# Joining the 64-row tail products of two DFT stages to passes that are row-tiled already, and spreading the filler work anew

## The chip, the core and the metric

The kernel runs on one core of a Trainium2 chip. The metric is the device time of one execution in microseconds (us); lower is better. The median of three runs of the kernel before is 507.38 us (507.01 to 507.38).

## What is computed

```python
xn = layernorm(x)                       # x: [2048, 576]
s  = irfft2(rfft2(xn) * (w_r + 1j*w_i)) # branch A
z  = gelu(xn @ w_in)                    # branch B, w_in: [576, 4608]
z1, z2 = z[:, :2304], layernorm(z[:, 2304:])
g  = w_sp @ z2 + b_sp[:, None]          # w_sp: [2048, 2048]
out = x + s * silu((z1 * g) @ w_out)    # w_out: [2304, 576]
```

## The kernel before

**Stages.** Rows of x come in 16 blocks of 128 (`m`). Branch A is a chain of small matrix products: p0 (row DFT, 16 blocks), then through DRAM p1 and p2/p3 (column DFT, filter, its inverse), p4 and p5 (inverse row DFT, 16 pieces `j`). Branch B makes z2 (96 chunks of 128 x 384, kept in SBUF, normalized there) and z1 (72 chunks of 128 x 512, sent to DRAM), and then the main products `w_sp @ z2` in a Strassen-like scheme of seven products (P1 to P7) a unit, 27 units, with the output products after each third of the rows. The main products begin with `tsum`, differences of normalized z2 blocks, and need `slab_sums`, sums and differences of four transposed slabs of w_sp.

**Filling.** The order on SP, PE (TensorE) and DVE (VectorE) is the program's own, written out by hand (`tc.manual_schedule`); ACT (ScalarE) and POOL (GpSimd) are ordered by the scheduler. `fill(n)` puts n z chunks between the steps of branch A, so that PE always has something to do; the string `kinds` says for each place whether it is a z2 chunk ("2") or a z1 chunk ("1"). `fill`'s second argument (`pace`) says how many items of the queue of z2 statistics and norms DVE takes after each chunk. After p5 come the chunks that are left, with the slab sums among them, and then `main`.

**Tails.** The inner dimension is 576 = 4 x 128 + 64. A chunk is four full-height products and one of 64 rows. Tails of four chunks are made together in one pass (place 1 of every four): two chunks are finished by it and two are begun by it, and partners lie in the upper and the lower 64 rows of the array, so two 64-row products can run beside one another. p0 and p5 have such a remainder too (288 = 2 x 128 + 32 rows, two parts; 289 = 2 x 128 + 33), but make it with a third product of full height, whose dead rows are zero in the tables (`live`, `seen`).

**Around the change, with lines.** `xpose` (L283) transposes a normalized block on PE (L287) and ACT copies it to `xnT` (L288). `p0_fold` (L292) adds and subtracts halves on DVE; `p0` (L297) makes six products (L302), ACT evacuates them (L304), POOL sends them to DRAM. Statistics of a block are `ln1` (L254: DVE L259/L260, reciprocal root on ACT for blocks 0 and 1, on POOL after that, `rstd_of` L248/L250), `ln1_apply` (L276/L279) normalizes it. z2 chunks are L410 on PE and L423/L429 on ACT; for the blocks in `ACT_SUMS` (4, 6, 8, 12, 14) ACT makes the sums for the norm too (a square over two chunks, L426). z1 chunks are L495/L504. `p5` (L381) has six products (L385), ACT and DVE evacuate (L388, L390, L391), POOL sends the piece to DRAM (L393). Norms are L466, slab sums L481 (one of the four, `SLB[6]`, on POOL for the first third), tsum L542/L544 on DVE and L546 on POOL. PSUM has four one-bank buffers for z chunks and transposes (`psh`) and two of two banks for branch A (`psa`).

Of the kernel before, what the change touches and what calls it, by code (L numbers as in the profile page):

```python
# [14 lines left out]
P = 128  # L15
# [8 lines left out]

def build_consts(S, D, L, LC0):
    tp = 2.0 * np.pi
    H = D // 2
    LE = L - L // 2
    d = np.zeros((3, P))
    live = np.ones((3, P))  # L30
    for b in range(2):
        d[b] = b * P + np.arange(P)
    nt_ = H - 2 * P
    d[2, 0:nt_] = 2 * P + np.arange(nt_)
    d[2, nt_:2 * nt_] = H + d[2, 0:nt_]
    live[2, 2 * nt_:] = 0.0
    cd = np.zeros((P, 2, 3, 2, LE))
    for par in range(2):
        l = 2 * np.arange(LE) + par
        ang = tp * ((d[:, :, None] * l) % D) / D * 1.0  # L40
        wt = live[:, :, None] * (l < L)
        cd[:, par, :, 0, :] = (np.cos(ang) * wt).transpose(1, 0, 2)
        cd[:, par, :, 1, :] = (-np.sin(ang) * wt).transpose(1, 0, 2)
    cd = cd.reshape(P, -1)

    s1 = np.arange(N1)
    k1 = np.arange(N1)
    lo, hi = k1 // N2, k1 % N2
    pos = [4 * hi + 2 * c + lo for c in range(2)]
    g1 = np.zeros((N2, P, P))  # L50
    g4 = np.zeros((N2, P, P))
    for s2 in range(N2):
        th = -tp * (((s1[:, None] * k1[None, :]) % N1) / N1 + s2 * k1[None, :] / S)
        co, si = np.cos(th), np.sin(th)
        for c, c2, v in ((0, 0, co), (1, 0, -si), (0, 1, si), (1, 1, co)):
            g1[s2, c * N1 + s1[:, None], pos[c2][None, :]] = v
        cot, sit = co.T, -si.T
        for c, c2, v in ((0, 0, cot), (1, 0, -sit), (0, 1, sit), (1, 1, cot)):
            g4[s2, pos[c][:, None], c2 * N1 + s1[None, :]] = v
    m2 = np.zeros((P, P))  # L60
    m3 = np.zeros((P, P))
    a = np.arange(N2)
    th = -tp * ((a[:, None] * a[None, :]) % N2) / N2
    co, si = np.cos(th), np.sin(th)
    for lo_ in range(2):
        for c, c2, v in ((0, 0, co), (1, 0, -si), (0, 1, si), (1, 1, co)):
            m2[c * N1 + lo_ * N2 + a[:, None], c2 * N1 + 2 * a[None, :] + lo_] = v
        for c, c2, v in ((0, 0, co), (1, 0, si), (0, 1, -si), (1, 1, co)):
            m3[c * N1 + 2 * a[:, None] + lo_, c2 * N1 + lo_ * N2 + a[None, :]] = v
    m3j = np.concatenate([m3[N1:], -m3[:N1]], axis=0)  # L70
    mm = np.stack([m2, m3, m3j], axis=1).reshape(P, 3 * P)

    ceso = np.zeros((P, len(LC0), 2, L))
    dd = np.arange(L)[None, :]
    seen = 0
    for i, l0 in enumerate(LC0):
        lv = (l0 + np.arange(P))[:, None]
        th = tp * ((lv * dd) % D) / D
        cl = np.where((lv == 0) | (lv == D // 2), 1.0, 2.0) * (lv >= seen) * 0.5 / (S * D)
        ceso[:, i, 0, :] = cl * np.cos(th)  # L80
        ceso[:, i, 1, :] = -cl * np.sin(th)
        seen = l0 + P
    return dict(cdsd=cd, g1=g1.transpose(1, 0, 2).reshape(P, N2 * P), g4=g4.transpose(1, 0, 2).reshape(P, N2 * P),
                mm=mm, ceso=ceso.reshape(P, -1))

@with_exitstack
def kernel(
# [23 lines left out]
    LC0 = [0, P, L - P]  # L111
    NLC = len(LC0)
# [6 lines left out]
    C = build_consts(S, D, L, LC0)  # L119
# [27 lines left out]
    nc.scalar.dma_start(out=ident[:], in_=cd_id.ap())  # L147
# [6 lines left out]
    nc.gpsimd.tensor_scalar(out=one[:], in0=one[:], scalar1=1.0, scalar2=1.0, op0=ALU.add, op1=ALU.mult)  # L154
# [59 lines left out]

    def load_x(c):
        t = AIN[c][:, 0:4 * D].rearrange("p (m d) -> p m d", m=4)
        if c == 0:
            for i in range(4):
                nc.sync.dma_start(out=t[:, i, :], in_=xv[:, i, :])
                if i == 1:  # L220
                    nc.sync.dma_start(out=CDSD, in_=cd_cdsd.ap().rearrange("p (a k l) -> p a k l", a=2, k=3))
        else:
            nc.sync.dma_start(out=t, in_=xv[:, 4 * c:4 * c + 4, :])
        return t
# [4 lines left out]
    def load_win(t, fs):  # L229
        for a in range(2):  # L230
            nc.sync.dma_start(out=t[:, a:KS - 1:2, :], in_=wv[a, 0:2 * P, fs].rearrange("(b p) f -> p b f", p=P))
        for q in range(4):
            nc.sync.dma_start(out=t[q * HT:(q + 1) * HT, KS - 1, :], in_=wv[q % 2, 2 * P:H2, fs])
# [6 lines left out]
    XC = [load_x(0)]  # L240
    for g in range(3):
        load_win(WIN2[:, :, 2 * g * ZC:2 * (g + 1) * ZC], slice(Fh + 2 * g * ZC, Fh + 2 * (g + 1) * ZC))
        XC.append(load_x(g + 1))
    nc.sync.dma_start(out=G1, in_=cd_g1.ap().rearrange("p (s k) -> p s k", s=N2))

    def rstd_of(mv, n, tag):
        ve = small.tile([P, n], F32, tag=tag + "v")
        nc.gpsimd.tensor_scalar(out=ve[:], in0=mv[:, :, 1], scalar1=1e-5, scalar2=1.0, op0=ALU.add, op1=ALU.mult)  # L248
# [4 lines left out]
    def ln1(ms):  # L253
        n = len(ms)  # L254
        mv = small.tile([P, n, 2], F32, tag=f"mv{n}", bufs=5)
        for i, m in enumerate(ms):
            st = small.tile([P, 2, 6], F32, tag="st1", bufs=4)
            for h in range(2):
                nc.vector.bn_stats(out=st[:, h, :], in_=XC[m // 4][:, m % 4, h * H2:(h + 1) * H2])  # L259
            nc.vector.bn_aggr(out=mv[:, i, :], in_=st[:])  # L260
        if ms[0] < 2:
            rs = small.tile([P, n], F32, tag=f"l1{n}r", bufs=5)
            nc.scalar.activation(out=rs[:], in_=mv[:, :, 1], func=ACT.Sqrt, bias=eps[:], scale=1.0)
            nc.vector.reciprocal(out=rs[:], in_=rs[:])
        else:
            rs = rstd_of(mv, n, f"l1{n}")
        for i, m in enumerate(ms):
            ln1_of[m] = (mv[:, i, 0:1], rs[:, i:i + 1])

    ln1_of = {}  # L270
# [26 lines left out]
    def p0(m):  # L297
        pa = psa.tile([P, 2, 512], F32, tag="a")
        for par in range(2):
            for k in range(3):  # L300
                lhs = FS[m % 4][:, par, k, :] if k < 2 else xnT[:, m, KS - 1, :]
                nc.tensor.matmul(pa[:, par, 0:2 * LE], lhsT=lhs, rhs=CDSD[:, par, k, :], start=(k == 0), stop=(k == 2))  # L302
        sg = PST[m % 8].rearrange("p (c l) -> p c l", c=2)
        nc.scalar.activation(out=sg.rearrange("p c (l a) -> p a c l", a=2),  # L304
                             in_=pa[:, :, 0:2 * LE].rearrange("p a (c l) -> p a c l", c=2), func=ACT.Identity)
# [59 lines left out]
    def p4(u):  # L365
        ch, lc = u // NLC, u % NLC
        av = AIN[ch].rearrange("p (s l) -> p s l", s=8)
        pa = psa.tile([P, 2, 4, P], F32, tag="a")
        for i in range(8):
            nc.tensor.matmul(pa[:, i // 4, i % 4, :], lhsT=av[:, i, LC0[lc]:LC0[lc] + P], rhs=G4[:, ch * 8 + i, :],  # L370
# [10 lines left out]
    def p5(j):  # L381
        pa = psa.tile([P, 2, 512], F32, tag="a")
        for c in range(2):
            for lc in range(NLC):
                nc.tensor.matmul(pa[:, c, 0:L], lhsT=V[:, lc, c, 2 * j:2 * j + 2, :], rhs=CESO[:, lc, c, :],  # L385
                                 start=(lc == 0), stop=(lc == NLC - 1))
        ob = THF[:, j % 2 * L:(j % 2 + 1) * L]
        nc.scalar.activation(out=ob, in_=pa[:, 1, 0:L], func=ACT.Identity)  # L388
        y = YST[j % 8]
        nc.vector.tensor_tensor(out=y[:, 0:L], in0=pa[:, 0, 0:L], in1=ob, op=ALU.add)  # L390
        nc.vector.tensor_tensor(out=y[:, L:D], in0=pa[:, 0, H2 - 1:0:-1], in1=ob[:, H2 - 1:0:-1], op=ALU.subtract)  # L391
        for h in range(2):
            nc.gpsimd.dma_start(out=Yv[2 * j + h], in_=y[h * N1:(h + 1) * N1, :])  # L393
# [77 lines left out]
    SA = dict(P1=4, P2=1, P5=2, P4=3, P6=0, P7=5, P3=6)  # L471
# [6 lines left out]
    def slab_sums(i, it):  # L478
        for o, a, b, op in ((5, 4, 2, ALU.subtract), (2, 2, 3, ALU.add), (0, 2, 4, ALU.subtract), (6, 1, 0, ALU.subtract)):
# [158 lines left out]
    kinds = "2" * (MT + 12) + "2221" * 4 + "2" * 12 + "12112111" * 6 + "21" * 12 + "2212" * 3 + "22112221"  # L638
# [11 lines left out]
    def fill(n, pace=1):  # L650
        for _ in range(n):
# [5 lines left out]
            if i % 4 == 1:  # L657
                done = held[:]
                held[:] = [chunk(i + 1), chunk(i + 2)]
                for r, c in enumerate(sorted(done + held, key=lambda c: c.wide)):  # L660
                    c.mm(KS - 1, slice(r % 2 * KT, (r % 2 + 1) * KT), c in held, c in done)
            elif i % 4 >= 2:
# [9 lines left out]
            z2_stats(pace)  # L672

    SP, PE, DVE = mybir.EngineType.SP, mybir.EngineType.PE, mybir.EngineType.DVE
    with tc.manual_schedule(engines={SP, PE, DVE}):
# [9 lines left out]
        ln1([0])  # L685
        ln1_apply(0)
        xpose(0)
        keep_warm(2)
        ln1([1])
        ln1_apply(1)  # L690
        nc.scalar.activation(out=THF[:, 0:1], in_=ln1_of[1][0], func=ACT.Gelu_apprx_tanh)
        p0_fold(0)
        xpose(1)
        ln1([2])
        p0(0)
        fill(1, 0)
        ln1_apply(2)
        p0_fold(1)
        fill(1, 0)
        xpose(2)  # L700
        p0(1)
        ln1([3])
        ln1_apply(3)
        fill(1, 0)
        nc.sync.dma_start(out=MM, in_=cd_mm.ap().rearrange("p (a k) -> p a k", a=3))
        ln1([4])
        for m in range(2, MT):
            if m + 1 < MT:
                xpose(m + 1)
            p0_fold(m)  # L710
            if m + 3 < MT:
                ln1([m + 3])
            if m + 2 < MT:
                ln1_apply(m + 2)
            fill(1, 0)
            p0(m)
# [5 lines left out]
        fill(11, 2)  # L722
        for s2 in range(0, N2, 2):
            p1(s2)
            fill(1)
# [6 lines left out]
        fill(12, 2)  # L732
        p2(0)
        for hh in range(0, N2, 2):
            fill(2)
            if hh + 2 < N2:
                p2(hh + 2)
            fill(1)
# [3 lines left out]
        fill(12, 2)  # L742
        for u in range(4 * NLC):
            p4(u)
            fill(1)
        for j in range(MT):
            p5(j)
            if j < 4 * NT // P:
                load_slab(0, (0, 2, 1, 3)[j % 4], j // 4)
            fill(1)  # L750
        load_z1(0)
        rest = kinds.rindex("2") + 1 - place[0]
        for i in range(NT // P):
            fill(rest // 4, 2)
            slab_sums(i, 0)
        fill(rest - 3 * (rest // 4), 3)
# [55 lines left out]
```

## Time and profile before

| | |
|---|---|
| time of the profiled execution | 507.27 us |
| its span on the core | 505.5 us |
| median of the runs | 507.38 us |
| PE, DVE, ACT, POOL busy | 98%, 65%, 34%, 43% of the span |
| p0 stage, waits for p1's input | until 41.5, until 50.7 us |
| p1; p2/p3; p4; p5 | from 50.7; 68; 147; 164 us |
| chunks that are left, after p5 | 191 to 212 us |
| main and output products | 212 to 500 us |

Busy times are unions of an engine's instructions. Matmuls are pipelined: an instruction lasts longer than its step, so what one costs is read from start to start in the timeline.

### The profile page before, as it was taken

The numbers are of one execution on the slowest core, as the hardware profiler recorded it, in microseconds if no ns is written. First come the engines' busy times: TensorE is split into PE (matmuls) and PEld (weight loads), VectorE is DVE, ScalarE is ACT, GpSimd is POOL, SyncE is SP. The second block draws the span as 40 slices with busy tenths as digits, with TensorE's granted clock in tenths as the row PEclk, the third lists the DMA queues.
The fourth block names the chain that finished last, engine by engine and source line by source line (L and its number), as shares of the span: only waits on it lengthen the run. The fifth ranks groups of instructions, "written<-read, shape, count | busy, mean of one in ns | idle before, by whom it ended". The sixth has DMA issues, their size and how long they took to land.

```text
span 505.5 us, 9339 instructions
## 1 busy us (share of the span) xinstructions
PE 497.5 (98%) x3454; PEld 313.8 (62%) x3454; DVE 329.6 (65%) x712; ACT 171.1 (34%) x356; POOL 217.5 (43%) x285
## 2 busy tenths in 40 slices
PE   7999999999999999999999999999999999999997
PEld 3565554444456664466666677666666678888885
DVE  5998887546355576766656547866665637877734
ACT  5887887556668666500000001100000011000001
POOL 2772243433332686754453511435445301666600
PEclk9999999999999999999999999999999999999999
DMA  8964869878573994381211399211121673111302
GB/s 257 333 180 132 281 216 325 248 209 238 164 267 93 178 276 151 126 272 33 63 32 47 92 169 209 75 47 48 31 64 31 150 140 120 34 43 44 88 18 79
DMA packets 85950, 70.82 MB, mean 140 GB/s; under 512 B 39760, under 2 KB 78416, under 8 KB 85648
## 3 DMA queue, kind: packets, MB, share of 16 engines
q1 hardware_dynamic: 80608, 56.08, 42.1%
q0 software_dynamic: 5152, 14.11, 8.4%
q8 instruction: 27, 0.44, 0.4%
q14 instruction: 19, 0.16, 0.1%
q10 hardware_dynamic: 144, 0.03, 0.0%
HBM read 40.55 MB, written 21.26 MB: 122 GB/s over the span
## 4 chain that ended last, share of the span: by engine, by line
PE 93%; DVE 4%; DMA 1%; issue 1%; ACT 1%; POOL 0%; SPq 0%; DVEq 0%; ACTq 0%
PE pm L558 43%; PE ph L495 14%; PE po L612 13%; PE ph L410 12%; PE pa L385 2%; PE pb L356 2%; PE pa L302 1%; PE pa L370 1%; PE pa L320 1%; PE pa L344 1%; PE pw L679 1%; DVE st L259 1%; DMA AR<-Ad 1%; PE pt L287 1%; DVE AR L276 1%
## 5 line engine op out<-in xcount | busy, mean ns | idle before, releaser
L558 PE MATMUL pm<-AR,Z_74 128*128 128x384 bf16 (+1 forms) x864 | 138.8, 308 | 0.0
L562 DVE TENSOR_TENSOR AR<-pm,AR 128x384 f32<-128x384 f32 (+3 forms) x162 | 82.5, 513 | 74.1 <-PE pm L558 70.0
L558 PEld LDWEIGHTS <-Z_74 128*128 128x128 bf16 x864 | 84.5, 98 | 40.6
L558 PE MATMUL pm<-AR 128*128 128x384 bf16 (+1 forms) x648 | 107.0, 308 | 0.1
L410 PE MATMUL ph<-AR 128*128 128x384 bf16 (+1 forms) x480 | 89.4, 327 | 0.5 <-DMA AR<-in_B_w_in_dram 0.4
L495 PE MATMUL ph<-AR 128*128 128x512 bf16 (+1 forms) x360 | 85.2, 379 | 0.0
L558 PEld LDWEIGHTS <-AR 128*128 128x128 bf16 x648 | 63.4, 98 | 30.7 <-issue 0.3
L572 ACT ACTIVATE AR<-pm 128x384 f32<-128x384 f32 (+1 forms) x27 | 12.3, 454 | 185.4 <-PE pm L558 185.4
L612 PE MATMUL po<-AR 128*128 128x288 bf16 x540 | 66.6, 286 | 0.0
L612 PEld LDWEIGHTS <-AR 128*128 128x128 bf16 x594 | 56.9, 98 | 13.9
L546 POOL TENSOR_TENSOR AR<-Z_74,AR 128x1024 bf16<-128x1024 bf16 x27 | 57.8, 2142 | 14.0 <-PE pm L558 12.1
L410 PEld LDWEIGHTS <-AR 128*128 128x128 bf16 (+1 forms) x480 | 39.8, 97 | 37.2 <-issue 17.7
L515 POOL DMA_DIRECT2D Z1d<-AR x58 | 32.9, 568 | 65.1 <-ACT AR L504 60.9
L573 POOL TENSOR_TENSOR AR<-AR 128x384 f32<-128x384 f32 (+1 forms) x27 | 22.8, 845 | 78.1 <-ACT AR L572 78.1
L504 ACT ACTIVATE AR<-ph 128x512 bf16<-128x512 f32 x72 | 42.5, 596 | 16.9 <-PE ph L495 14.1
L495 PEld LDWEIGHTS <-AR 128*128 128x128 bf16 (+1 forms) x360 | 30.5, 97 | 28.5 <-issue 4.6
L429 ACT ACTIVATE Z_74<-ph 128x384 bf16<-128x384 f32 x66 | 30.8, 492 | 20.0 <-PE ph L410 19.8
L615 ACT ACTIVATE TH<-po 128x576 f32<-128x576 f32 x15 | 9.8, 651 | 77.8 <-PE po L612 77.8
L576 POOL TENSOR_TENSOR AR<-AR 128x384 f32<-128x384 f32 (+1 forms) x27 | 30.3, 1123 | 11.8 <-DVE AR L562 11.8
L569 DVE TENSOR_TENSOR AR<-AR 128x384 bf16<-128x384 bf16 (+1 forms) x108 | 31.7, 335 | 0.9
L346 DVE TENSOR_TENSOR AR<-pa,AR 128x578 bf16<-128x578 f32 x32 | 22.7, 751 | 13.6 <-PE pa L344 13.6
L621 DVE SCALAR_TENSOR_TENSOR AR<-TH,po 128x576 bf16<-128x576 f32 x15 | 11.3, 752 | 29.9 <-ACT TH L615 29.9
(105 smaller groups left out, 492.1 us busy)
## 6 DMA issues: line engine op xcount, KB each, us to landing
Z1d<-AR POOLq DMA_DIRECT2D x58, 128.0 KB, 3.5
AR<-Z1d SPq DMA_DIRECT2D x36, 192.0 KB, 3.0
AR<-in_A_x_dram SPq DMA_DIRECT2D x20, 144.0 KB, 2.9
AR<-in_B_w_out_dram SPq DMA_DIRECT2D x1, 2592.0 KB, 10.4
Ad<-AR POOLq DMA_DIRECT2D x16, 144.5 KB, 4.3
AR<-Ad SPq DMA_DIRECT2D x4, 578.0 KB, 5.8
AR<-in_A_w_r_dram SPq DMA_DIRECT2D x16, 144.5 KB, 4.2
AR<-in_A_w_i_dram SPq DMA_DIRECT2D x16, 144.5 KB, 4.1
```

The costliest lines, as they stand in the source:

```text
L410: nc.tensor.matmul(self.ph[:], lhsT=xnT[rows, self.m, ks, :], rhs=WIN2[rows, ks, n * ZC:(n + 1) * ZC], start=start, stop=stop)
L429: nc.scalar.activation(out=zc, in_=ph[:], func=ACT.Gelu_apprx_tanh)
L495: nc.tensor.matmul(self.ph[:].rearrange("p (a t) -> p a t", a=4), lhsT=wb[rows, ks, (fi % WG) * P:(fi % WG + 1) * P], rhs=xnT[rows, 4 * tq ...
L504: nc.scalar.activation(out=zs, in_=ph[:], func=ACT.Gelu_apprx_tanh)
L515: (nc.sync if place[0] > len(kinds) - 16 else nc.gpsimd).dma_start(out=d, in_=s_)
L546: nc.gpsimd.tensor_tensor(out=t, in0=zblk(p, 1, 0), in1=t2, op=ALU.subtract)
L558: nc.tensor.matmul(dst, lhsT=z[:, s, :], rhs=SLB[SA[name]][:, s, 0:nt], start=(s == 0 and not more), stop=(s == HM - 1), skip_group_check= ...
L562: nc.vector.tensor_tensor(out=out, in0=x, in1=y, op=ALU.add)
L569: nc.vector.tensor_tensor(out=o, in0=o, in1=zb[:, f, h, 0:nt], op=ALU.mult)
L573: nc.gpsimd.tensor_tensor(out=p1b, in0=p1, in1=B[1], op=ALU.add)
L576: nc.gpsimd.tensor_tensor(out=ux, in0=p1a, in1=B[0], op=ALU.add)
L612: nc.tensor.matmul(pv[:, hh, :], lhsT=U[:, fi, h, i * P:(i + 1) * P], rhs=WOUT[:, fi, c0 + hh * H2:c0 + hh * H2 + w // nh], start=(fi == 0 ...
```

## The change

- The third products of p0 and p5 are gone. p0's remainder of block m (two 64-row products) and of block m+1 are made in one tail pass of the z chunks (`p0_pair`); for an even block the pass ends its sum, for an odd one it begins it. p5's remainders of two pieces (`p5_tails`) are made in such a pass and begin their sums. The tables hold the remainder twice, in both halves of the rows; p4 writes V's third block to match, and the order of p5's pieces and of the rows of `Yv` follows.
- p0 gets two fills a block (32 chunks for 17), p5 two a piece (34 for 16); every fourth step of p1 and p2/p3 and every third of p4 loses its own. `kinds` and the paces are new.
- At the start x's first 512 rows come in three transfers, the first third of `w_in`'s z2 half is issued ahead of the DFT table, half of it from ACT's queue; the first two z2 chunks stand ahead of p0's first product, the statistics of blocks 1 to 3 earlier.
- Slab sums are rewritten (the same four results, other places): two of the four need no buffer of p5 and are made within p5's end, the other two behind p5.

```diff
+    def p0_tail(m, start):
+        if start:
+            p0_ps[m] = psa.tile([P, 2, 512], F32, tag="a", name="pa")
         for par in range(2):
-            for k in range(3):
-                lhs = FS[m % 4][:, par, k, :] if k < 2 else xnT[:, m, KS - 1, :]
-                nc.tensor.matmul(pa[:, par, 0:2 * LE], lhsT=lhs, rhs=CDSD[:, par, k, :], start=(k == 0), stop=(k == 2))
+            rows = slice(par * KT, (par + 1) * KT)
+            nc.tensor.matmul(p0_ps[m][:, par, 0:2 * LE], lhsT=xnT[rows, m, KS - 1, :], rhs=CDSD[rows, par, 2, :],
+                             start=start, stop=not start, skip_group_check=True)
+    def p0(m, start):
...
+        for par in range(2):
+            for k in range(2):
+                nc.tensor.matmul(p0_ps[m][:, par, 0:2 * LE], lhsT=FS[m % 4][:, par, k, :], rhs=CDSD[:, par, k, :],
+                                 start=start and k == 0, stop=not start and k == 1, skip_group_check=True)
...
+    def p5_tails(js):
+        for j in js:
+            p5_ps[j] = psa.tile([P, 2, 512], F32, tag="a", name="pa")
         for c in range(2):
-            for lc in range(NLC):
+            for j in js:
+                rows = slice(j // 2 % 2 * KT, (j // 2 % 2 + 1) * KT)
+                nc.tensor.matmul(p5_ps[j][:, c, 0:L], lhsT=V[rows, 2, c, 2 * j:2 * j + 2, :], rhs=CESO[rows, 2, c, :],
+                                 start=True, stop=False, skip_group_check=True)
...
-    SA = dict(P1=4, P2=1, P5=2, P4=3, P6=0, P7=5, P3=6)
+    SA = dict(P1=4, P2=1, P5=0, P4=3, P6=5, P7=2, P3=6)
...
+    def slab_sums(i, it, part=None):
+        ops = ((0, 2, 3, ALU.add), (2, 4, 2, ALU.subtract), (5, 0, 4, ALU.subtract), (6, 1, 5, ALU.subtract))
+        for o, a, b, op in ops if part is None else ops[:2] if part == 0 else ops[2:]:
...
-    kinds = "2" * (MT + 12) + "2221" * 4 + "2" * 12 + "12112111" * 6 + "21" * 12 + "2212" * 3 + "22112221"
+    kinds = "2" * 32 + "221" * 11 + "21" * 33 + "2111" * 7 + "2121"
...
+        def p0_pair(m):
+            p0_tail(m, False)
+            p0_tail(m + 1, True)
+            p0_out(m)
...
         for m in range(2, MT):
-            if m + 1 < MT:
+            if m % 2 == 0:
                 xpose(m + 1)
             p0_fold(m)
             if m + 3 < MT:
-                ln1([m + 3])
+                ln1(m + 3)
             if m + 2 < MT:
                 ln1_apply(m + 2)
+            p0(m, m % 2 == 0)
+            if m % 2:
+                p0_out(m)
             fill(1, 0)
-            p0(m)
+            if m % 2 and m + 1 < MT:
+                xpose(m + 1)
+            fill(1, 0, (lambda: p0_pair(m)) if m % 2 == 0 else None)
...
-        for j in range(MT):
-            p5(j)
-            if j < 4 * NT // P:
-                load_slab(0, (0, 2, 1, 3)[j % 4], j // 4)
-            fill(1)
+        for n in range(0, MT, 2):
+            while place[0] % 4 != 1:
+                fill(1, 0.8)
+            fill(1, 0.8, lambda: p5_tails(js[n:n + 2]))
+            p5(js[n], n)
...
+            fill(1, 0.8)
+            p5(js[n + 1], n + 1)
+            fill(1, 0.8)
+            if n % 4 == 2 and n >= 10:
+                slab_sums((n - 10) // 4, 0, 0)
+        slab_sums(2, 0, 0)
         load_z1(0)
-        rest = kinds.rindex("2") + 1 - place[0]
         for i in range(NT // P):
-            fill(rest // 4, 2)
-            slab_sums(i, 0)
-        fill(rest - 3 * (rest // 4), 3)
+            fill(1, 2)
+            slab_sums(i, 0, 1)
+        fill(max(kinds.rindex("2") + 1 - place[0], 0), 2)
```

## The prediction

> **What bounds the kernel now.** I read the page first: the busy times and the chain that ended last.
>
> ```profile
> span 505.5 us, 9339 instructions
> PE 497.5 (98%) x3454; PEld 313.8 (62%) x3454; DVE 329.6 (65%) x712; ACT 171.1 (34%) x356; POOL 217.5 (43%) x285
> ...
> PE 93%; DVE 4%; DMA 1%; issue 1%; ACT 1%; POOL 0%; SPq 0%; DVEq 0%; ACTq 0%
> ```
>
> TensorE (PE) is never idle for long, so a product saved anywhere is time saved, but a wait opened anywhere is time lost in full. So the order of work matters more than any engine's sum. The table by stage shows where there is room (columns: stretch, its length, busy us of PE, PEld, DVE, ACT, POOL, then granted clock, DMA share, GB/s).
>
> ```profile
> 6.00:12.00 6.00, 4.44 (x30) 2.10 (x29) 4.12 (x16) 4.46 (x8) 1.64 (x3) 1.00 1.03 327
> 18.00:24.00 6.00, 5.97 (x51) 3.72 (x49) 5.90 (x23) 5.16 (x9) 4.40 (x10) 1.00 1.03 326
> 198.00:212.00 14.00, 14.00 (x69) 5.56 (x68) 12.78 (x16) 8.04 (x15) 10.87 (x11) 1.00 0.42 140
> ```
>
> The p0 stage (to 42 us) has VectorE (DVE) full and ScalarE (ACT) at 86%. In the 14 us before the main products PE only fills while DVE and GpSimd (POOL) work hard: slab sums, last norms. That stretch is cover.
>
> **Tail products.** The step prices come from PE's timeline of the p0 stage.
>
> ```profile
> 21.82 0.91 PE L302 MATMUL pa<-AR 128*128 128x290 bf16 x6
> 22.57 0.44 PE L287 MATMUL pt<-ident,AR 128*128 128x128 bf16 x5
> 22.85 0.81 PE L410 MATMUL ph<-AR 128*128 128x384 bf16 x4
> 23.50 0.91 PE L302 MATMUL pa<-AR 128*128 128x290 bf16 x6
> ...
> 26.81 1.31 PE L410 MATMUL ph<-AR 128*128 128x384 bf16 x8
> 28.05 0.92 PE L302 MATMUL pa<-AR 128*128 128x290 bf16 x6
> ```
>
> From start to start: six p0 products 0.75 (0.125 each), five transposes 0.28, four z products 0.65. Four z products with a tail pass take 28.05 - 26.81 = 1.24, so the pass costs 0.59 for four 64-row products: one after the other they alone would take 0.65, so they run in pairs, two times 0.16, and 0.26 is entry and exit. The change adds two pairs of 290 columns to a pass that exists already: 0.26 with the few ns between partners, for four full-height products of 0.125 = 0.50. That is -0.24 a pass; p0 has 8 such passes, p5 (289 columns, same step) 8: **-3.8 us**. Bounds: -4.0 if pairs are free of any extra, 0 if the partners ran one after the other; the z pairs are the nearest row, so -3.8.
>
> **The start.** Now PE's issue loses 7.5 us up to 7.8 us (all but one block's transposes, 0.28) and, adding up each start's excess over its step to 36 us, another 3.1: 0.54 waiting for w_in at 9.0, 0.41 and 0.71 for DVE at 14.5 and 15.7, the rest small; the stretch 6:12 above is where most of it lies. After: half of the first w_in third is issued on ACT's queue ahead of the identity and of ACT's table load, so it shares the DMA engines with x (until now x alone): I put x 0.4 later. Then DVE's chain (statistics 0.82, aggregate, root, apply 0.7) puts the first transposes at 5.6 to 6.0 and z chunk 0 at 7.2, against 9.0. ACT's table load (1.28) moves to about 2.2 to 3.5, still ahead of the root at 4.6. GpSimd now takes the variances of blocks 1 and 2 before either power (0.55 each), so block 1 is applied only at 8.2 to 8.7 (0.25 of PE's time). On SP the row DFT's table moves behind four w_in issues of 0.58: issued at 4.4, 4.4 to land, 8.8, needed at 9.1. Another 0.67 goes in the first tail pass, where chunk 3 has its PSUM buffer from block 2's transposes, which ACT empties only at 10.8. Lost in all 7.2 - 0.28 + 0.25 + 0.67 = 7.85, against 10.6: **-2.8** (-1 to -4; the DMA sharing is the unknown).
>
> **The p0 loop, the first new wait.** Per pair of blocks PE now has 32 chunks instead of 17 to fill with, and no longer waits for DVE's 1.9 us a block. But the built order of the changed kernel shows a loop: tail pass, then on ACT two gelus, the p0 evacuation of the even block, that of the odd one, a gelu, and only then the evacuation of the next even block's transposes, which DVE's fold reads and p0 of that block needs. PE has only one chunk and one set of transposes (0.93 us) between those transposes and that p0; now it has a whole block (1.9 us). ACT's rows:
>
> ```profile
> 22.35 0.50 ACT L429 ACTIVATE Z_74<-ph 128x384 bf16<-128x384 f32 x1
> 22.77 0.82 ACT L304 ACTIVATE AR<-pa 128x580 bf16<-128x580 f32 x1
> 23.45 0.69 ACT L288 ACTIVATE AR<-pt 128x640 bf16<-128x640 bf16 x1
> 24.02 0.50 ACT L429 ACTIVATE Z_74<-ph 128x384 bf16<-128x384 f32 x1
> ```
>
> Steps: gelu 0.42, p0 0.68. Counted from the pass's start: ACT begins at 0.36; 2 x 0.42 + 2 x 0.68 + 0.42 + 0.69 = 3.31, so 3.67, and DVE's first fold 0.28 gives 4.0. PE is there at 0.70 (pass) + 0.50 + 0.65 + 0.28 + 0.65 + 0.28 = 3.06. Wait 0.95, for blocks 4 to 12: 5 x 0.95 = 4.75. Chunks 24 to 29 belong to block 4, whose sums ACT makes itself: three reads of 0.09 and a square of 0.82 more (its rows' steps) ahead of block 14: 2.0. **+6.8**, from +1 (if ACT's steps shrink) to +8. Behind the wait stand that p0, the next chunks and all later evacuations; nothing else feeds PE. The read of Ad, 7.8 us after the last evacuation as now, lies behind 13 chunks instead of 11; it saves about 0.1 of the 0.38 lost today.
>
> The Trainium skill, TensorEngine Tiling (Array Packing), PSUM Bottleneck, speaks against the change: tiling quickens TensorE, not the emptying of PSUM. This case's rows put ACT at 4.1 us a pair against PE's 4.95, so its rate would allow the gain and only its order doesn't; were the rule binding by rate, the p0 half of the saving (1.9) would be gone too.
>
> **p1 to p4.** Every fourth p1, p2 and third p4 loses its chunk, so two products that share two PSUM buffers follow directly. Evacuations there take 0.65 to 1.2 with ACT over 80% busy. Today these waits are 0.3 in all; the eight or nine bare places may cost 0 to 0.3 each: **+1.0** (0 to 2.5). p5's passes need both buffers 2.9 us after the last p5, whose evacuation takes 1.5: nothing. Moving stores and slab loads within p5 hides behind 32 chunks.
>
> **The entry into the main products, the second new wait.** Today 20 us of chunks stand between p5's last product (191.3) and main (211.9). After, p5 uses them up: behind it PE has five z1 chunks (four products of 0.216 each) and one pass (0.64), 4.95, then P1 (8 x 0.1625 = 1.3), and P6 would start at 6.25. P6 reads a difference of all normalized z2 blocks and slab 5. Behind p5's last output on DVE (done at 1.45) the order holds: statistics 0.46, seven slab sums of 0.61, aggregate 0.23, the last norm 0.78, the difference 0.64: 6.4, so 7.85. POOL meanwhile has three slab sums, the third difference, then the addition that P4 waits for. Its rows and what they do to DVE today, at the end of the covered stretch:
>
> ```profile
> 203.28 4.89 POOL L481 TENSOR_TENSOR AR<-AR 128x1024 bf16<-128x1024 bf16 x2
> ...
> 201.47 2.12 DVE L481 TENSOR_TENSOR AR<-AR 128x1024 bf16<-128x1024 bf16 x3
> 203.51 2.68 DVE L466 TENSOR_SCALAR Z_74<-Z_74,mv,rs 128x2304 bf16<-128x2304 bf16 x1
> ```
>
> POOL: 5.5 (root ready) + 3 x 2.45 + 2.14 + 0.9 = 15.9, and DVE's addition 0.5: P4 at 16.4 against 6.25 + 4 x 1.3 = 11.45. So 5.0 even if DVE runs freely. It doesn't: a norm of 0.87 (group mean 0.98) took 2.68 beside POOL's sums. At that rate the difference ends at 11.8 or 13.8, by who starts first, and P4 at 17.4 or 19.0. So 5.0 to 7.5; **+6.3**. The cover for this was the stretch 198:212 shown above.
>
> The Trainium skill, SBUF — State Buffer, Who interferes with whom, says that such a pair excludes one another for whole instructions. The row disagrees in part: under a full block the norm could not have ended at 206.19, 0.46 after POOL's first sum. By the rule the difference would end near 14.4 and this term would be 8.1.
>
> **Sum.** -3.8 - 2.8 + 6.8 - 0.1 + 1.0 + 6.3 = +7.4. The profiled execution took 507.27 (span 505.5 and 1.8 around it), the median is 507.38: the same within 0.02%. Forecast 514.7.
>
> **Rivals.** *Covered after all (faster):* if ACT reached the even block's transposes within 0.93 us of them and DVE and POOL were done at main's entry, only the saving and the start remain: 507.3 - 3.8 - 2.8 - 0.1 = 500.6, up to 506. It decides at a loop wait under about 1.1 us a pair together with an entry wait under 1. For it: ACT's and DVE's sums have room. Against: both waits follow from in-order queues. 0.13. *One of the two waits only:* loop alone 507.3 - 6.7 + 6.8 + 0.5 = 507.9; entry alone 507.4. 0.14; half of it within 0.2%. *Worse:* pairs that don't overlap (no saving: 518.5), or DVE wholly blocked with p1 to p4 at their bound: 518 to 521. 0.10. *The forecast,* all three terms in their bounds: 508.5 to 518. 0.63.
>
> **How the numbers follow.** Range 507.5 to 519.0: it leaves out the covered case and the far end of the worse one. 0.2% (1.0 us) is about what a measurement of this kernel can tell from no change. Faster 0.13 (covered), same 0.07 (half of one wait only), slower 0.80.
>
> **What would show it.** Right: in p0's stage PE waits of about 1 us for DVE's fold ahead of every even block's p0, ACT behind it; p1 reached near 63 us; at main's entry PE waits for the DVE difference and then the POOL one, 5 us or more; tail passes of p0 with eight products in about 0.85. Wrong: PE busy in every slice from 16 us to the end, or no gap in the first ten us of main. If passes with eight tails take over 1.1, the pairs don't overlap.

## The result and the profile after

The changed kernel takes **519.73 us** (median of four runs, 518.54 to 520.20) against 507.38 in the same comparison: 2.4% slower, ratio 1.024 (95% interval 1.0221 to 1.026). The forecast was 514.7 with a range of 507.5 to 519.0. So the direction was right, and the time lies 0.73 us beyond the range. Measured once more, beside a later run, the same kernel took 518.93 in the median, just inside it. The profiled execution took 518.54 (span 516.8), at the fast end of its runs, and the differences below are against its 507.27 before.

From the page of the changed kernel, the span and busy times, the granted clock in 40 slices, and the chain that ended last:

```profile
span 516.8 us, 9330 instructions
PE 495.7 (96%) x3454; PEld 313.3 (61%) x3454; DVE 331.7 (64%) x711; ACT 170.7 (33%) x355; POOL 223.1 (43%) x288
...
PEclk8999999999999999979999999999999999999999
...
PE 87%; ACT 5%; DVE 3%; DMA 2%; issue 1%; ACTq 0%; POOL 0%; DVEq 0%; POOLq 0%
```

PE's sum is hardly smaller (495.7 against 497.5 us), although the tail products got cheaper, and 87% instead of 93% of the chain is PE's. The loss has three places: the first 14 us, the p0 stage, and slices 17 and 18, main's entry. In the first and the last the granted clock drops too. The table by stage (stretch, its length, busy us of PE, PEld, DVE, ACT, POOL, granted clock, DMA share, GB/s):

```profile
6.00:12.00 6.00, 4.11 (x22) 2.26 (x23) 4.54 (x16) 0.76 (x3) 1.56 (x4) 0.72 0.97 288
218.00:224.00 6.00, 1.89 (x6) 0.89 (x7) 5.97 (x4) 0.00 (x0) 5.37 (x4) 0.61 0.64 194
```

Before, the clock column read 1.00 in all three stretches that the prediction shows.

**The start.** PE's timeline: the transposes of block 0 wait for the identity, a transfer of 32 KB issued at 1.74 us behind two of 384 KB on the same queue; then eight z products take 2.30 us instead of 1.46.

```profile
7.89 0.69 PE L284 MATMUL pt<-ident,AR 128*128 128x128 bf16 x5 [2.85 <-DMA ident<-c_id]
...
9.38 2.30 PE L433 MATMUL ph<-AR 128*128 128x384 bf16 x8
...
14.02 0.67 PE L309 MATMUL pa<-AR 128*128 128x290 bf16 x4
```

**The p0 stage,** one pair of blocks (start, us, engine, line; the last bracket is idle time and what ended it):

```profile
40.02 1.89 PE L433 MATMUL ph<-AR 128*128 128x384 bf16 x12
...
42.09 0.67 PE L309 MATMUL pa<-AR 128*128 128x290 bf16 x4
...
42.54 1.51 ACT L314 ACTIVATE AR<-pa 128x580 bf16<-128x580 f32 x2
...
44.22 0.76 ACT L285 ACTIVATE AR<-pt 128x640 bf16<-128x640 bf16 x1
...
45.02 0.29 DVE L291 TENSOR_TENSOR AR<-AR 128x256 bf16<-128x256 bf16 x1 [1.99 <-ACT AR L285]
...
45.36 0.36 PEld L309 LDWEIGHTS <-AR 128*128 128x128 bf16 x4 [0.92 <-DVE AR L291]
...
45.37 0.67 PE L309 MATMUL pa<-AR 128*128 128x290 bf16 x4 [0.75 <-ACT Z_74 L452]
```

The z products of two chunks and the pass with eight tails run from 40.02 to 42.09: 2.07 - 8 x 0.1625 = 0.77. In the kernel before, a pass of four z tails of 384 columns took 0.53 in six of eleven cases (the others have gaps in them), so the four p0 tails cost about 0.24. In p5's stage passes take 0.88 with p5's four tails, and 0.63 with the same z tails alone before: 0.25. Then ACT works off two p0 evacuations and a gelu before it reaches the transposes at 44.22; DVE's fold follows, and p0 at 45.37. From start to start PE issues nothing for 0.90 to 0.92 us here in blocks 4 to 12, and 1.98 in block 14. The bracket at p0 names a gelu, which ends at 45.37 too, as p0 starts. But the row of PEld shows the real wait: p0's first weights are what the fold wrote, and loading them waits for the fold (45.02 + 0.29) and begins at 45.36.

**Main's entry.** P6 behind its wait, and what DVE and POOL did in it; P1 had started at 214.49:

```profile
222.11 2.74 PE L582 MATMUL pm<-AR 128*128 128x384 bf16 x8 [6.16 <-DVE AR L566]
...
216.26 2.67 DVE L489 TENSOR_SCALAR Z_74<-Z_74,mv,rs 128x2304 bf16<-128x2304 bf16 x1 [0.73 <-POOL rs L243]
218.85 2.60 DVE L505 TENSOR_TENSOR AR<-AR 128x1024 bf16<-128x1024 bf16 x1
221.37 0.68 DVE L566 TENSOR_TENSOR AR<-Z_74 128x1024 bf16<-128x1024 bf16 x1
...
216.20 4.70 POOL L505 TENSOR_TENSOR AR<-AR 128x1024 bf16<-128x1024 bf16 x2
```

The last norm (0.87 alone) takes 2.67 and a slab sum (0.61 alone) 2.60 beside POOL's sums, as foreseen. Eight products of P6 take 2.74 instead of 1.46. P4 starts at 229.28, that is 14.79 after P1; five products of 1.3 would be 6.5.

### The profile page after: what moved, and what is told of

It is laid out like the page before. It is cut to its first block, busy times and chain, and to the rows that moved or that the text cites. A ratio compares the mean times of both kernels' runs of the same rounds, so it can differ in the third digit from the quotient of the medians.

```text
span 516.8 us, 9330 instructions
## 1 busy us (share of the span) xinstructions
PE 495.7 (96%) x3454; PEld 313.3 (61%) x3454; DVE 331.7 (64%) x711; ACT 170.7 (33%) x355; POOL 223.1 (43%) x288
## 4 chain that ended last, share of the span: by engine, by line
PE 87%; ACT 5%; DVE 3%; DMA 2%; issue 1%; ACTq 0%; POOL 0%; DVEq 0%; POOLq 0%
PE pm L582 42%; PE po L636 13%; PE ph L519 12%; PE ph L433 12%; PE pa L407 2%; PE pb L366 2%; ACT AR L314 1%; PE pa L309 1%; ACT Z_74 L452 1%; DMA ident<-c_id 1%; PE pa L381 1%; PE pa L354 1%; ACT AR L285 1%; DMA Bd<-AR 1%; DVE Z_74 L489 1%
## 5 line engine op out<-in xcount | busy, mean ns | idle before, releaser
L582 PE MATMUL pm<-AR 128*128 128x384 bf16 (+1 forms) x648 | 108.3, 311 | 6.3 <-DVE AR L566 6.2
L433 PE MATMUL ph<-AR 128*128 128x384 bf16 (+1 forms) x480 | 90.8, 329 | 0.7 <-ACT AR L285 0.4
L636 PE MATMUL po<-AR 128*128 128x288 bf16 x540 | 66.6, 286 | 0.0
L433 PEld LDWEIGHTS <-AR 128*128 128x128 bf16 (+1 forms) x480 | 41.2, 97 | 37.9 <-issue 15.9
L570 POOL TENSOR_TENSOR AR<-Z_74,AR 128x1024 bf16<-128x1024 bf16 x27 | 57.9, 2145 | 11.3 <-PE pm L582 11.2
L539 POOL DMA_DIRECT2D Z1d<-AR x59 | 34.5, 586 | 60.1 <-ACT AR L528 58.8
L519 PEld LDWEIGHTS <-AR 128*128 128x128 bf16 (+1 forms) x360 | 30.5, 97 | 28.6 <-issue 5.2
L452 ACT ACTIVATE Z_74<-ph 128x384 bf16<-128x384 f32 x66 | 32.0, 499 | 25.6 <-PE ph L433 25.3
L645 DVE SCALAR_TENSOR_TENSOR AR<-TH,po 128x576 bf16<-128x576 f32 x15 | 11.3, 754 | 30.0 <-ACT TH L639 26.8
```

What stands on the lines that cost most here:

```text
L433: nc.tensor.matmul(self.ph[:], lhsT=xnT[rows, self.m, ks, :], rhs=WIN2[rows, ks, n * ZC:(n + 1) * ZC], start=start, stop=stop)
L452: nc.scalar.activation(out=zc, in_=ph[:], func=ACT.Gelu_apprx_tanh)
L519: nc.tensor.matmul(self.ph[:].rearrange("p (a t) -> p a t", a=4), lhsT=wb[rows, ks, (fi % WG) * P:(fi % WG + 1) * P], rhs=xnT[rows, 4 * tq ...
L539: (nc.sync if place[0] > len(kinds) - 16 else nc.gpsimd).dma_start(out=d, in_=s_)
L570: nc.gpsimd.tensor_tensor(out=t, in0=zblk(p, 1, 0), in1=t2, op=ALU.subtract)
L582: nc.tensor.matmul(dst, lhsT=z[:, s, :], rhs=SLB[SA[name]][:, s, 0:nt], start=(s == 0 and not more), stop=(s == HM - 1), skip_group_check= ...
```

## The experiments

All are edits of the changed kernel, compared with the kernel before on the same chip. The kernel before took 507.04 to 507.17 in these comparisons, so medians from different chips can be set side by side to a few tenths. The changed kernel itself was measured twice, 519.73 and, in the last section but one of the experiments, 518.93; its own runs lie almost 2 us apart, so small differences are read from the traces. "P1 to P4" is the time between the starts of these two products of the first unit.

### The start: identity first

```diff
+    nc.scalar.dma_start(out=ident[:], in_=cd_id.ap())
     for g in range(3):
...
         if g == 0:
-            nc.scalar.dma_start(out=ident[:], in_=cd_id.ap())
```

> The changed kernel, but the 32 KB of the identity are issued on ACT's queue ahead of the two 393 KB transfers of w_in instead of behind them. Theory (the first transposes wait for the identity, which waits for w_in, and the idle time costs half the TensorE clock besides): first transposes at 5.6 to 6.0 us instead of 7.89, no stretch at clock 0.5, z chunk 0 near 7.2 instead of 9.38, p0 of block 1 near 11.5 instead of 14.02; 519.7 falls by 2.5 to 3.2, to about 516.8. Rival (the rows of x and DVE's statistics are the real bound of the start, the identity only came last by a little): less than 1.0 us. Second rival (the clock falls in any case, since TensorE stays idle from 4.7 to 6): about 1.5.

Measured 519.12 (518.53 to 521.01): no gain that can be told from the changed kernel. The identity landed 2.1 us after its issue instead of 6.1, the transposes came at 5.33, and then other transfers were late (PE's and DVE's timeline):

```profile
8.87 0.82 DVE L250 BATCH_NORM_STATS2 st<-AR 128x6 f32<-128x288 bf16 x2 [2.76 <-DMA AR<-in_A_x_dram]
9.30 1.30 PE L433 MATMUL ph<-AR 128*128 128x384 bf16 x7 [2.17 <-DMA AR<-in_B_w_in_dram]
```

The theory falls: the identity was only the first in a row. w_in came at 9.30 and x's blocks 2 and 3 at 8.87 (7.54 in the changed kernel); in the profiled execution p0 of block 1 started at 15.21, and products ran at half clock up to 17.58. Why x landed later than in the changed kernel stays open.

### The start: transfers in the order of use

```diff
-    for m0, m1 in ((0, 1), (1, 2), (2, 4)):
+    for m0, m1 in ((0, 1), (1, 2)):
...
+            nc.sync.dma_start(out=XC[0][:, 2:4, :], in_=xv[:, 2:4, :])
...
-        keep_warm(2)
+        keep_warm(6)
         fill(1, 0)
-        ln1(2)
         ln1_apply(1)
         p0_fold(0)
+        ln1(2)
```

(with the identity first; the third transfer of x now stands behind w_in's remainders.)

> The changed kernel with the identity ahead of w_in on ACT's queue, the third transfer of x (blocks 2 and 3, 288 KB) behind the w_in remainders instead of ahead of them, the statistics of block 2 on DVE behind the fold of block 0, and six instead of two idle-time products of 512 columns ahead of z chunk 0. In the run with the identity alone first, z chunk 0's second product waited for w_in until 9.30 us and the statistics of block 2 for x until 8.87. Theory (the start is bound by the order of the transfers on shared DMA engines; the identity is only the first in a row): w_in is there by 7.5, chunk 0 is through at 8.8, p0 of block 1 starts near 11.7 instead of 14.0 to 15.2, no stretch at clock 0.5 in the first 16 us: 2.0 to 3.0 us less than the changed kernel. Rival (w_in's 768 KB take until 9 whatever stands ahead of them): p0 of block 1 no earlier than 13.2, less than 1.0 us.

Measured 517.76 (517.06 to 519.12), 1.2 to 2.0 us below the changed kernel's two medians. Chunk 0 is made from 7.34, with 0.2 us of wait in it and at full clock (7.2 had been forecast), so the order of the transfers is what held it. But p0 of block 1 starts at 12.94, not 11.7: the DFT table now comes late, and block 2 follows its x.

```profile
7.34 1.66 PE L434 MATMUL ph<-AR 128*128 128x384 bf16 x8
...
9.80 0.66 PE L310 MATMUL pa<-AR 128*128 128x290 bf16 x4 [0.52 <-DMA AR<-c_cdsd]
...
12.94 0.67 PE L310 MATMUL pa<-AR 128*128 128x290 bf16 x4
```

### The loop: p0 of even blocks behind a chunk

```diff
-            p0(m, m % 2 == 0)
             if m % 2:
+                p0(m, False)
                 p0_out(m)
             fill(1, 0)
+            if m % 2 == 0:
+                p0(m, True)
```

> The changed kernel, but p0 of an even block stands behind the first chunk of its block instead of ahead of it, so that PE has four z products (0.65 us) more between the transposes of that block and its p0. Theory (the wait is one of order: ACT reaches the evacuation late, at a fixed time from the pass): the wait of 0.91 falls to about 0.25 in blocks 4 to 12 and from 1.98 to 1.3 in block 14; in all -4.0 us, between -3.0 and -4.5. Rival (ACT's or DVE's rate bounds the loop, so the wait turns up at the next place, for a PSUM buffer or at the pass): within 1.0 us of the changed kernel's 519.7.

Measured 514.84 (514.66 to 515.36); span 513.1 against 516.8. The idle time is 0.26 in blocks 4 to 12, and 1.05 ahead of a chunk and 0.28 ahead of p0 in block 14: 5 x 0.65 + 0.65 = 3.9 us gone, as the theory had it. One such block, four z products and then p0 (0.92 from start to start, of which 0.65 are the products):

```profile
41.85 0.81 PE L433 MATMUL ph<-AR 128*128 128x384 bf16 x4
...
42.77 0.67 PE L309 MATMUL pa<-AR 128*128 128x290 bf16 x4
```

Moving only the place of p0 in PE's order, with ACT's work unchanged, removes over half of the loop's loss of 6.5 us: that part is order, not rate.

### The loop: block 4's sums on DVE

```diff
-    ACT_SUMS = (4, 6, 8, 12, 14)
+    ACT_SUMS = (6, 8, 12, 14)
```

(on top of the edit above.)

> The changed kernel with p0 of even blocks behind a chunk (as in the run before, 514.84) and, besides, the sums for block 4's norm on DVE instead of ACT. Theory (the longer wait at block 14, 1.05 us ahead of a chunk and 0.28 ahead of p0 with that edit, is ACT's own work for those sums): the 1.05 goes, 513.8. Rival (it is ACT's backlog, or DVE gets too full behind it): 514.8 or more.

Measured 512.79 (511.50 to 513.37), 2.05 below the run without this line. The 1.05 is gone, and block 14 waits 0.26 like the others. One more us than expected went too, partly between p1 and p2; that part wasn't followed.

### The pairs: partners on the same rows

```diff
-            rows = slice(par * KT, (par + 1) * KT)
+            rows = slice(0, KT)
             nc.tensor.matmul(p0_ps[m][:, par, 0:2 * LE], ...)
```

> The changed kernel, but p0's tail products all use the lower 64 rows of xnT and of the table (both halves hold the same values), so that partners no longer lie in different rows. Theory (pairs run side by side; but ACT's evacuations, which set the wait ahead of the next even block's p0, count from the start of the pass): an eight-tail pass takes 0.25 more (1.03 instead of 0.78), the wait of 0.91 behind it falls by as much, and the time stays within 0.6 us of the changed kernel. Rival 1 (the two are independent): 2.0 us more. Rival 2 (partners never overlapped): neither pass nor wait changes.

Measured 518.28 (517.94 to 519.00). PE's timeline, with the pass and the wait behind it:

```profile
40.33 1.90 PE L433 MATMUL ph<-AR 128*128 128x384 bf16 x12
...
42.64 0.67 PE L309 MATMUL pa<-AR 128*128 128x290 bf16 x4
...
45.66 0.55 PE L309 MATMUL pa<-AR 128*128 128x290 bf16 x3 [0.49 <-ACT Z L452]
```

From 40.33 to 42.64 are 2.31, so the pass takes 1.01, 0.24 more than with partners in different rows: the pairs do overlap. The idle time ahead of p0 is 0.66 instead of 0.91, and the time is no longer than the changed kernel's. So the half of the tail saving that falls to p0 is real, and in the five pairs with this wait it buys nothing while ACT's order sets the pair's length. p5's passes were not changed here.

### The entry: POOL's slab sums on DVE

```diff
-            (nc.gpsimd if o == 6 and it == 0 else nc.vector).tensor_tensor(out=SLB[o]...
+            nc.vector.tensor_tensor(out=SLB[o]...
```

> The changed kernel, with the three slab sums of GpSimd (2.45 us each) on DVE (0.61 each). Theory (the entry is late because GpSimd's sums stretch DVE's norm and last sum from 0.87 and 0.61 to 2.67 and 2.60, and hold GpSimd's own difference and additions back): norm 0.9, P6 at 219.5 instead of 222.1, P4 at 224.7 instead of 229.3; -4.6 us (-3.5 to -5.0). Rival (the last norm is bound by its statistics and root, 216.2, and DVE with three sums more is no earlier): P6 at 221 or later, less than 1.5 us.

Measured 516.43 (516.15 to 516.74). The norm took 0.87, as the theory said; POOL's sums had stretched it. P6 starts at 220.45, P1 to P4 is 12.88 instead of 14.79: 1.9 of the 4.6 us expected. P6 is 0.95 later than expected, by the three sums more on DVE and then POOL's addition beside the difference. The other 1.7 are lost behind P6: from there to P4 are 6.89 instead of 4 x 1.3, because P6 and the next product ran partly at half clock after the wait (the clock's record has 0.5 from 220.97 to 224.39):

```profile
216.87 0.87 DVE L489 TENSOR_SCALAR Z<-Z,mv,rs 128x2304 bf16<-128x2304 bf16 x1
...
218.71 1.13 POOL L597 TENSOR_TENSOR AR<-AR 128x384 f32<-128x384 f32 x1 [2.66 <-issue]
218.99 1.40 DVE L566 TENSOR_TENSOR AR<-Z 128x1024 bf16<-128x1024 bf16 x1
...
220.45 2.26 PE L582 MATMUL pm<-AR 128*128 128x384 bf16 x8 [4.53 <-DVE AR L566]
```

### The entry: the clock

```diff
         nc.gpsimd.tensor_tensor(out=p1b, in0=p1, in1=B[1], op=ALU.add)
+        if u == 0:
+            pd = psa.tile([P, 2, 512], F32, tag="a", name="pd")
+            for r in range(3):
+                prod(pd[:, r % 2, 0:nt], "P1", zblk(p, 0, 0))
         prod(b, "P6", tb[u, 0])
```

(`range(3)` in the first run, `range(5)` in the second.)

> The changed kernel, with 24 products more (P1 of the first unit made three times over into a buffer that nobody reads, 3.9 us) in the wait ahead of the first P6. Theory (the whole difference at the entry between forecast and trace is the halved clock): P6 still at about 222.1, its wait 2.4 instead of 6.3, the clock stays 1.0, and the 12 products that took 0.32 instead of 0.16 give back 2.0 us. Rival (P4 would have waited in any case, for the additions that GpSimd makes at 226.5 to 228.8, so the slow products only fill that wait): 0.4 us, with a new wait of 1.5 ahead of P4.

Measured 518.11 (517.68 to 518.39). TensorE was still idle for 2.43 us, and the clock fell all the same, for one step. Two stretches of this kernel's table by stage, cut where the clock changed:

```profile
219.30:222.72 3.42, 1.16 (x8) 0.51 (x7) 3.38 (x3) 0.00 (x0) 2.79 (x2) 1.00 0.58 152
222.72:226.13 3.41, 3.41 (x12) 1.57 (x11) 3.41 (x3) 0.00 (x0) 3.41 (x2) 0.50 1.09 372
```

So this run couldn't decide, and the wait was filled to its end:

> The changed kernel with 40 products more (P1 of the first unit made five times over, 6.5 us) ahead of the first P6: the whole wait is filled. With 24 of them TensorE was still idle for 2.4 us and 11 products took 0.32 each. Theory 1 (the clock costs what the slow products add beyond GpSimd's additions): no product slow, P6 at 222.2, P4 waits for the additions until about 228.5: 0.8 us less than the profiled changed kernel (518.5), and the runs lie closer together than that kernel's 518.5 to 520.2, since the place of the 3.4 us steps of the clock no longer matters. Theory 2 (the clock costs its full 2.0 us): P4 at 227.4, 2.0 us less.

Measured 517.97 (517.32 to 518.94). No product of the entry was slow, P6 had a gap of 0.23 us, and P4 had one of 0.84: P1 to P4 is 14.06 against 14.79. P6 and P4:

```profile
223.43 1.46 PE L582 MATMUL pm<-AR 128*128 128x384 bf16 x8
...
229.69 1.46 PE L582 MATMUL pm<-AR 128*128 128x384 bf16 x8 [0.68 <-DVE AR L586]
```

Theory 1 holds: at the entry the clock costs 0.7 us of the profiled execution, since GpSimd's additions would have held P4 anyway. The runs did not draw together as it expected (1.6 us apart). The start was unchanged, and the profiled execution had half clock up to 13.80 us, against 11.1 in the changed kernel's; the run with both waits filled, below, tests that.

### The entry: its cover put back

```diff
-        for o, a, b, op in ops if part is None else ops[:2] if part == 0 else ops[2:]:
+        for o, a, b, op in ops if part is None else ops[:2] if part == 0 else ops[part + 1:part + 2]:
...
-            (nc.gpsimd if o == 6 and it == 0 else nc.vector).tensor_tensor(out=SLB[o]...
+            nc.vector.tensor_tensor(out=SLB[o]...
...
-    kinds = "2" * 32 + "221" * 11 + "21" * 33 + "2111" * 7 + "2121"
+    kinds = "2" * 32 + "221" * 11 + "21" * 42
...
             slab_sums(i, 0, 1)
-        fill(max(kinds.rindex("2") + 1 - place[0], 0), 2)
+        while stats_q or norm_q:
+            tick[0] += 1
+            z2_stats(1)
+        for w in (0, 2, 1):
+            tsum(0, w)
+        for i in range(NT // P):
+            slab_sums(i, 0, 2)
...
-        for w in (0, 2, 1):
-            tsum(0, w)
```

(Part 1 of `slab_sums` is now slab 5 alone, part 2 is slab 6, and both are on DVE.)

> The changed kernel with the cover put back at main's entry: the last z2 chunk at place 148 instead of 162 of 168 (z1 chunks behind it), so that all norms are done within p5; behind p5 DVE makes slab 5's three sums, then the three differences, then slab 6's three sums, which GpSimd had. Theory (the entry costs 8.3 us because the last norm, slab 5 and the first difference come one after the other behind p5): P6 without a wait or with one under 1.5 us, no clock 0.5; 7.0 to 8.3 us less, about 512. Rival (slab 5 can't be written before p5's last pieces have left its place, so its sums and P6 stay late): P6 2.5 us late or more, 4 to 5 us less.

Measured 513.52 (513.20 to 514.74), 5.4 to 6.2 us less, between the two expectations. P6 waits 0.2, as the theory said. But P7 now waits 2.9 for the addition that reads P6's result, because slab 6's sums stand before it on DVE and take 1.5 each beside POOL. P1 to P4 is 9.91.

```profile
215.71 1.47 PE L582 MATMUL pm<-AR 128*128 128x384 bf16 x8 [0.21 <-DVE AR L566]
...
216.30 4.54 DVE L505 TENSOR_TENSOR AR<-AR 128x1024 bf16<-128x1024 bf16 x3
...
221.35 1.46 PE L582 MATMUL pm<-AR 128*128 128x384 bf16 x8 [2.87 <-DVE AR L586]
```

### TensorE kept busy through both waits

```diff
-            for j in range(5):
+            for j in range(11):
                 nc.tensor.matmul(pw[:], lhsT=warm[:, 0:P], rhs=warm, start=True, stop=True)
```

(at the very start, and the 40 products ahead of P6.)

> The changed kernel with TensorE kept busy through both long waits: 22 instead of 10 products of 512 columns at the very start, until the identity is there, and the 40 products of the earlier run ahead of the first P6. All waits for data stay. Theory (what the forecast lacked at the start is part late transfers and part the halved clock, and where the clock's 3.4 us steps fall is chance): no step at 0.5 after the first one at full clock, p0 of block 1 at 12.7 to 13.2 instead of 14.0; the time 516.3 to 516.9 in the median and its runs within 0.7 us of one another, where the changed kernel's four lay 1.7 apart. Rival (the spread comes from the transfers, not from the clock): median 517.5 or more and runs as far apart as before.

> The changed kernel once more, on the same chip as the run above, for the spread of its runs and as its yardstick: 518.5 to 520.2, as before.

Measured 516.90 (516.70 to 516.96) for the first and 518.93 (518.40 to 520.35) for the changed kernel beside it. With extra work and no wait for data removed, the kernel is 2.0 us faster, and its runs lie 0.26 us apart instead of 1.95: the spread comes from the clock. The table by stage of the first:

```profile
6.00:12.00 6.00, 5.64 (x43) 3.18 (x41) 4.41 (x16) 1.60 (x4) 1.55 (x4) 1.00 0.96 286
218.00:224.00 6.00, 6.00 (x39) 3.61 (x38) 5.96 (x5) 0.00 (x0) 5.37 (x3) 1.00 0.62 199
```

p0 of block 1 starts at 13.09 here; in the profiled executions of the changed kernel at 14.02 and at 15.21. P1 to P4 is 14.05.

The second of those two shows a trap. Its clock column reads 1.00 for the stretch in which eight z products take 2.74 us instead of 1.46 (0.32 from start to start instead of 0.16), because its first record of the clock comes only at 13.8 us:

```profile
6.00:12.00 6.00, 4.32 (x18) 2.23 (x19) 4.33 (x15) 0.96 (x3) 1.54 (x4) 1.00 0.92 282
...
9.16 2.74 PE L433 MATMUL ph<-AR 128*128 128x384 bf16 x8
```

### What paid, together

The start's order, p0 behind a chunk, block 4 on DVE, and the entry with the two early slab sums moved ahead of p5's last pieces and slab 6 behind main's first addition:

```diff
             fill(1, 0.8)
+            if n >= 10:
+                slab_sums((n - 10) // 2, 0, 0)
             p5(js[n + 1], n + 1)
...
+        for w in (0, 2):
+            tsum(0, w)
         for i in range(NT // P):
             fill(1, 2)
             slab_sums(i, 0, 1)
+        tsum(0, 1)
+        later.append(lambda: [slab_sums(i, 0, 2) for i in range(NT // P)])
```

> The changed kernel with the edits that paid put together: the start's transfers in the order of use; p0 of even blocks behind a chunk; block 4's sums on DVE; the last z2 chunk at place 148; within p5's end the two slab sums that need no buffer of p5, ahead of the last pieces' sums on DVE; behind p5 the first difference, slab 5's three sums on DVE, and slab 6's three sums behind the first addition of main. Theory (three separate losses: start 2.0, loop 6.9, entry 7.5, that add up): 503 to 504.5, faster than the kernel before (507.1). Rival (they hide one another, or DVE is too full in the one place left): 506 or more, no faster than before.

Measured **505.29** (504.39 to 506.10): ratio to the kernel before 0.9961 (0.9947 to 0.9975), faster than that kernel by 0.4% and than the changed one, though 0.8 us short of what was expected. From its page and its waits of TensorE:

```profile
span 502.7 us, 9327 instructions
PE 493.4 (98%) x3458; PEld 311.4 (62%) x3458; DVE 331.9 (66%) x719; ACT 168.0 (33%) x343; POOL 211.8 (42%) x278
...
PE pm L583 <- DVE AR L587: 1.1, 1, 1.1
```

PE is back at 98%, and of the waits at the entry 1.1 us ahead of P4 and 0.5 ahead of P6 are left. So with its waits closed the changed kernel comes out ahead. How much of that is due to the pairs is not shown: the kernel before was not run with the new start or with block 4's sums on DVE, and this one not without pairs.

## Where the prediction was right, and where it was wrong

| step | forecast | profiled execution | with TensorE kept busy |
|---|---|---|---|
| tail products | -3.8 | 16 x -0.25 = -3.9 | the same |
| start | -2.8 | -2.8 + (14.02 - 11.33) = -0.1 | -2.8 + (13.09 - 11.33) = -1.0 |
| p0 loop | +6.8 | 5 x 0.91 + 1.98 = +6.5 | the same |
| p1 to p4 | +1.0 | 1.5 of gaps against 0.3: +1.2 | about the same |
| entry | +6.3 | 14.79 - 6.5 = +8.3 | 14.05 - 6.5 = +7.6 |
| sum (forecast also has -0.1 for Ad) | +7.4 | +12.0 | +10.4 |
| measured | | +11.3 | +9.7 |

14.02 and 13.09 are the measured starts of p0 of block 1, and 11.33 is where the prediction's own terms put it: z chunk 0 at 7.2, eight z products 1.30, two sets of transposes 0.56, four p0 products 0.50, a pass 0.85, and the two losses of 0.25 and 0.67. The steps make 0.7 us more than the difference of the times, in both columns; where that 0.7 comes back wasn't followed.

- **Right:** the price of a pair, and the loop, to 0.3 us: the wait stands where it was put, behind ACT's order, and the run with p0 behind a chunk shows that it is the order. (The pass read at 0.59 held 0.06 of wait; that leaves the price of the added pairs as it is.) The rival *covered after all* fell by the entry, 6.3 us against the 1 it allowed; its sign for the loop, a wait under 1.1, would not have told it from the forecast's own 0.95, and 0.91 was measured. The rival *worse* named 518 to 521, where the median lies, but by other causes: the pairs do overlap, the gaps in p1 to p4 are 1.5 us in all, and DVE was not wholly blocked (below). The part of that rival with pairs that don't overlap is refuted by the run on the same rows, which also shows that its price would have been too high by p0's half.
- **Wrong, the clock:** every product was priced at its full-clock step, though the prediction itself had TensorE wait 5.5 to 7.5 us for P6 at the entry, and again at the start. The sum has no term for it. That alone is enough to leave the range: the changed kernel with TensorE kept busy takes 516.9, within it. In the profiled execution the clock costs 0.9 at the start and 0.7 at the entry (at the start 2.1 in the second one, 15.21 - 13.09), and 2.0 in the median of the runs. But the range was left by 0.73 only, and by their sizes either of the next two terms, had it been right, would have kept the time inside; that one median lies outside and the other just inside is chance, within the spread of the runs.
- **Wrong, the start** (mis-sized by 1.8 without the clock): z chunk 0 was put at 7.2 because DVE and ACT are ready then. The step took the identity as there and allowed 0.4 us for x; the identity's own issue line, behind two large transfers on one queue, was read but only for the sharing. It landed at 7.8 (6.1 from its issue). With the transfers in the order of use chunk 0 starts at 7.34, so the engines' part of that step was right.
- **Wrong, the entry** (mis-sized by 1.3 without the clock): P6's part was good: the difference ends at 222.05, 12.5 after p5's products end (209.53); 11.8 or 13.8 had been worked out. For P4 the text gave 17.4 or 19.0 and the sum took less; 4.95 + 14.05 = 19.0 is what came. The estimate of 14.4 for the difference, by the full block of the Trainium skill, SBUF — State Buffer, Who interferes with whom, was 1.9 too late. The trace again shows no full block: the norm ended at 218.93, 0.62 after POOL's first sum (216.20 to 218.31), and it takes 0.87 alone. The 8.1 for the whole term that went with that estimate is nearer the 7.6 and 8.3 measured than 6.3 is, but for another reason: P4 waits for an addition on DVE that waits for one of POOL's.
- "p1 near 63" came at 66.6: 2.7 of it is the start; the rest was not followed.

## What to carry to other kernels

A wait that a forecast opens on TensorE has two prices: its length, and slower products behind it if the stretch is long; look in the profile for the clock column and the start-to-start times of the products as well as for the wait, and if runs of one kernel lie further apart than another's, suspect the same. Filler work that is spent on one stage is taken from another, so say for each stage what covers it after the change. A small transfer that everything needs must not stand behind large ones, but moving one transfer ahead gains only as much as the next late one allows.

## What the runs showed of the hardware that was not expected

The granted clock of TensorE fell to 0.5 in steps of 3.41 us or two of them (6.83). After the 6.3 us wait at the entry products of 384 columns took 0.32 us from start to start instead of 0.16. A wait with 2.43 us without products brought one such step, beginning at 222.72; one of 3.0 us in the run with the entry's cover put back (218.3 to 221.35) brought none. Counted on in steps of 3.41 from 11.10, where its last step at half clock ended, that run has a step's end at 219.3, which parts the 3.0 into 1.0 and 2.0; the 2.43 (219.59 to 222.02) lies within one step, 219.30 to 222.72. So where the idle time falls on the steps would explain the difference; two waits don't show it.

The Trainium skill, TensorE: Matmul & The Clock Gate, Part 1: The HAM clock gate, describes a free-running window of about 3.4 us, an idle one halving the clock and a busy one restoring it. The step lengths and the chance between runs agree. Its rule of thumb there (HAM oscillation — how this bites in real kernels), no idle gaps over about 3.4 us, is not safe by these runs: the 2.43 us wait, shorter than a window, was enough.
